# First four attention units: score copies on DVE, results split straight from PSUM, w_out's words queued behind the gates'

## Chip, cores, metric

One Trainium2 chip, one core of it. The metric is the device time of one execution in microseconds; runs are compared by their medians.

## The reference, cut

```python
def _attn_ref(q, k, v, n_sink, window):          # 4 x 8 heads, 768 positions, 64 wide; n_sink 4, window 128
    scores = q @ k.T / sqrt(64), kept where key < n_sink or 0 <= row - key < window
    return softmax(scores) @ v
def _moe_ref(x, w1, w2, w3, w_out):              # x 3072 x 512, gates 512 x 768, w_out 768 x 512
    h = np.maximum(np.maximum(x @ w1, x @ w2), x @ w3)
    return h @ w_out
# then routing of 3072 tokens to 8 experts of 384 each (argsort of all logits), and per expert relu(x @ w1) @ w2
```

## The kernel before

Everything is one instruction stream per engine, laid out by a list scheduler that takes the operations in program order with priorities; each engine then runs its list in order.

**Attention** is cut into 32 units (4 batches, 2 halves of the rows, 4 pairs of heads); four units make a group of 384 tokens. A unit is loaded (`load`), prepared (`prep`), scored (`score`), softmaxed (`soft`) and multiplied with the values (`pv`). The first eight units are "native": their scores are plain fp32 matmuls of queries QF against keys KZ, without the high and low parts of `prep`. In `score` a unit has three blocks of rows and two heads: TensorE (PE) writes a score tile `ps` (three buffers in PSUM), ACT copies it into the score tile T (L134), DVE overwrites the part that the mask selects (L135). The tile for the first block of a first-half unit is preset by POOL (L114) and only DVE writes it (L130, L131). `soft` takes the maximum on DVE (L141), six exponentials on ACT (L144) and scales on POOL (L147, "the weighting"). In `pv`, PE transposes the tile (L25: `pt` for the sink columns, `pp` for the window of each head), DVE multiplies with the triangular masks into A (L163), ACT and DVE split the sink part (`psb`, L153 and L154), and PE accumulates `po` (L170, L172; one buffer). ACT copies `po` to SBUF as x (L173).

**The first mixture** (`Moe1.group`) splits x of each unit into fp32r high and low parts `xh`, `xl` (L267 on ACT, L268 on DVE) and multiplies them with three gates (L280, three products each; maxima on L282 and L283). x2 (L305) multiplies with w_out. The float64 weights arrive as pairs of 32-bit words and are put together by `single` (L220 load, L226 on ACT, L225 and L227 on DVE, L228 on POOL) and split (L212 on ACT, L213 on POOL). The 18 gate pieces pass through a ring of four slots in the storage named HL; the six w_out pieces use two tiles named `st`. Group 0's h is spilled to DRAM and reloaded later by `reload` (L321; split by L323 on ACT and L324 on DVE) before its x2.

Names in rows: until w_out is loaded its storage (`woh`, `wol`) lends room to the attention (`Spare`), so `woh<-in_k_dram` is a native unit's keys and `T_w` or `wol<-ps` is a score tile T. `kz` are the low parts of keys of later, non-native units. SP issues the loads (SPq), in its own order; POOL sets zeros in the unused halves of the key tiles (L53).

The second mixture, with its routing on DVE, begins after about 600 us and is not touched.

Of the kernel before, what the change touches and what calls it, by code (L numbers as in the profile page):

```python
# [22 lines left out]
def f32(ap): return ap.bitcast(FT)  # L23
def flip(nc,out,x,ident):
    nc.tensor.transpose(out,x,f32(ident))  # L25

class Attn:
    def __init__(s, tc, q,k,v,vs, keep, consts, pst, psp, pss, psv, work):
        s.tc=tc; s.nc=nc=tc.nc; s.q,s.k,s.v,s.vs=q,k,v,vs
        s.pst,s.psp,s.pss,s.psv,s.w=pst,psp,pss,psv,work  # L30
        jp=work.tile([128,128],I32,name="jp",tag="qs0",bufs=2)
        nc.gpsimd.iota(jp,pattern=[[1,128]],base=0,channel_multiplier=-1)
        s.ident=keep.tile([128,128],FR,name="ident")
        nc.vector.tensor_scalar(s.ident,jp,0.0,None,op0=OP.is_equal)
        s.ca=consts.tile([128,2,128],U8,name="ca")
        nc.vector.tensor_scalar(s.ca[:,0,:],jp,0.0,None,op0=OP.is_le)
        nc.vector.tensor_scalar(s.ca[:,1,:],jp,0.0,None,op0=OP.is_gt)
        s.ul=consts.tile([128,2,128],BF,name="ul")
        nc.vector.tensor_scalar(s.ul[:,0,:],jp,0.0,None,op0=OP.is_lt)
        nc.vector.tensor_scalar(s.ul[:,1,:],jp,0.0,None,op0=OP.is_ge)  # L40
        s.negs=consts.tile([128,2,4],FT,name="negs"); nc.vector.memset(s.negs,NEG)

        s.vk=[]; s.pb=[]
        for i in range(2):
            t=consts.tile([128,2,128],FR,name=f"vk{i}"); nc.vector.memset(f32(t),0.0); s.vk.append(t)
            t=consts.tile([128,384],FR,name=f"psb{i}"); nc.vector.memset(f32(t),0.0); s.pb.append(t)
        s.kf=[]; s.kz=[s.zeros([consts.tile([128,4,132],FR,name=f"kz{h}") for h in range(2)])]
        t=consts.tile([1,1],FT,name="one"); nc.vector.memset(t,0.0)
        nc.scalar.activation(t,t,AF.Exp)
        s.n=0; s.no=('kh0','kh1')  # L50
        s.extra=None
# [58 lines left out]
    def score(s,u):  # L110
        nc=s.nc; w=s.w; hf=u['hf']
        T=s.two(u,[128,6,132],FT,"T",3)
        u['T']=T
        if hf==0: nc.gpsimd.memset(T[:,0:2,:],NEG)  # L114
        for i in range(3):
            first = hf==0 and i==0
            if first: lo,n=0,132
            else: lo,n=(i-1+hf)*132,260
            t=T[:,2*i:2*i+2,:].rearrange("p u j -> p (u j)")
            for h in range(2):  # L120
                ps=s.pss.tile([128,512],FT,name="ps")
                iq=slice(i*128,(i+1)*128); kz=u['KZ'][h].rearrange("p c j -> p (c j)")[:,lo:lo+n]
                if u['nat']: nc.tensor.matmul(ps[:,:n],u['QF'][:,iq],kz,start=True,stop=True)  # L123
                else:
                    kh=u['KH'][h].rearrange("p c j -> p (c j)")[:,lo:lo+n]
                    nc.tensor.matmul(ps[:,:n],u['QS'][h][:,iq],kh,start=True,stop=False)  # L126
                    nc.tensor.matmul(ps[:,:n],u['QS'][h][:,iq],kz,start=False,stop=True)  # L127
                block=t[:,136*h:136*h+128]; sink=t[:,128+4*h:132+4*h]
                if first:
                    nc.vector.copy_predicated(block,s.ca[:,0,:],ps[:,0:128])  # L130
                    nc.vector.copy_predicated(sink,s.ca[:,1,0:4],ps[:,128:132])  # L131
                else:

                    nc.scalar.activation(t[:,132*h:132*h+132],ps[:,128*h:128*h+132],AF.Copy)  # L134
                    nc.vector.copy_predicated(block,s.ca[:,h,:],ps[:,132-132*h:260-132*h])  # L135
            if hf==0 and i==1:
                nc.vector.copy_predicated(t[:,128:136].rearrange("p (h j) -> p h j",h=2),s.ca[:,1,0:4][:,None,:].to_broadcast([128,2,4]),s.negs)
# [10 lines left out]
    def pv(s,u,x):  # L148
        nc=s.nc; w=s.w; T=u['T'].rearrange('p u j -> p (u j)'); hf=u['hf']; nb=u['nb']; nat=u['nat']
        psk=s.pst.tile([128,512],FT,name="pt")  # L150
        for i in range(3): flip(nc,psk[:,i*128:(i+1)*128],T[:,264*i+128:264*i+256],s.ident)
        PB=s.pb[u['n']%2]
        nc.scalar.activation(PB[0:8],psk[0:8,:384],AF.Copy)  # L153
        nc.vector.tensor_tensor(PB[32:40],psk[0:8,:384],f32(PB[0:8]),op=OP.subtract)  # L154
        jobs=[]
        if hf: jobs.append((0,128,0,0))
        for i in range(3): jobs.append((i*256+128,256 if i<2 else 128,i*128,i+hf))
        for h in range(2):
            pt=s.psp.tile([128,512],FT,name="pp")
            for i in range(3):  # L160
                flip(nc,pt[:,i*128:(i+1)*128],T[:,i*264+136*h:i*264+136*h+128],s.ident)
            A=s.two(dict(n=u['n']*2+h),[128,3,2,128],FT,"A")
            nc.vector.tensor_tensor(A,pt[:,:384].rearrange("p (i q) -> p i q",q=128)[:,:,None,:].to_broadcast([128,3,2,128]),  # L163
                s.ul[:,None,:,:].to_broadcast([128,3,2,128]),op=OP.mult)
            Af=A.rearrange("p i u q -> p (i u q)")
            a=slice(64*h,64*h+64); o=slice(64-64*h,128-64*h)
            if nat:
                if h==0:
                    po=s.psv.tile([128,512],FT,name="po")
                    for a_ in range(2): nc.tensor.matmul(po[:,:384],u['VK'][:,a_,:],PB,start=(a_==0),stop=False,skip_group_check=True)  # L170
                for c,n,q,blk in jobs:
                    nc.tensor.matmul(po[a,q:q+n],u['vn'][:,blk,h,:],Af[:,c:c+n],start=False,stop=True,skip_group_check=True)  # L172
                if h==1: nc.scalar.activation(x,po[:,:384],AF.Copy)  # L173
                continue
            H=w.tile([128,768],FR,name="H"); L=w.tile([128,768],FR,name="L")
            nc.scalar.activation(H,Af,AF.Copy)  # L176
            nc.gpsimd.tensor_tensor(L,Af,f32(H),op=OP.subtract)  # L177
            po=s.psv.tile([128,512],FT,name="po")
            for part in (H,L):
                for j,(c,n,q,blk) in enumerate(jobs):  # L180
                    nc.tensor.matmul(po[:,q:q+n],u['VS'][:,blk,128*h:128*h+128],part[:,c:c+n],start=(part is H and j==0),stop=False,skip_group_check=True)  # L181
            nc.tensor.matmul(po[:,:384],u['VK'][:,h,:],PB,start=False,stop=True,skip_group_check=True)
            nc.scalar.activation(x[a,:],po[o,:384],AF.Copy)
            nc.vector.tensor_tensor(x[a,:],po[a,:384],x[a,:],op=OP.add)

class Spare:

# [15 lines left out]
class Moe1:  # L203
    def __init__(s, tc, words,wgate, consts, wpool, main, conv, mm, pt, pss, ident):
        s.tc=tc; s.nc=tc.nc; s.mm=mm; s.pss=pss; s.main=main; s.conv=conv; s.ident=ident; s.consts=consts
        s.src=words; s.wgate=wgate
        s.W=[[wpool.tile([128,4,768],FR,name=f"w{i}{x}") for x in "hl"] for i in range(3)]
        s.WO=None; s.at=None; s.stage=None; s.HL=None; s.n=0
        s.WG=main.tile([128,6,16],FR,name="wgt")
    def split(s,src,hi,lo):  # L210
        nc=s.nc
# [2 lines left out]
    def single(s,src,ring=False):  # L214
# [2 lines left out]
        if ring and s.stage is None: s.stage=s.main.tile([128,12,384],FT,name="HL").rearrange("p a b -> p (a b)").bitcast(I32)  # L217
        if ring: st=s.stage[:,s.n%4*1024:(s.n%4+1)*1024].rearrange("p (n t) -> p n t",t=2)
        else: st=s.conv.tile([128,512,2],I32,name="st",bufs=2)
        nc.sync.dma_start(st.rearrange("p n t -> p (n t)"),src.bitcast(I32))  # L220
        A=s.pss.tile([128,512],FT,name="ps").bitcast(I32); C=st[:,:,0]
        if ring and s.n%3==2: R=s.stage[:,4096:4608]
        else: R=s.conv.tile([128,512],I32,name="cA",bufs=2)
# [3 lines left out]
        nc.vector.scalar_tensor_tensor(R,st[:,:,1],-0x40000000,A,op0=OP.bitwise_and,op1=OP.bitwise_or)  # L227
        nc.gpsimd.tensor_tensor(R,R,C,op=OP.add)  # L228
        return R.bitcast(FT)
    def part(s,x,f):  # L230
        return s.HL[:,"hl".index(x)*6+f]
    def load_w(s,f):
# [27 lines left out]
    def group(s,xs,spill=None,pool=None,mid=None,between=None):  # L260
# [1 line left out]
        nc=s.nc; main=s.main  # L262
        X=[]
        for p in range(4):
            h=main.tile([128,384],FR,name=f"xh{p}",bufs=1); l=main.tile([128,384],FR,name=f"xl{p}",bufs=1)
            with s.tc.high_priority():
                nc.scalar.activation(h,xs[p],AF.Copy)  # L267
                nc.vector.tensor_tensor(l,xs[p],f32(h),op=OP.subtract)  # L268
            X.append((h,l))
        H=[]  # L270
        if s.HL is None and spill is None: s.HL=main.tile([128,12,384],FR,name="HL")
        for f in range(6):
# [351 lines left out]
def attention_mixtures(tc,q,k,v,vs,words,wg,u1,u2,out,off=60,spread=(0,1,3,4),native=8,order='a0 a0 a0 a0 w a1 w a1 w w a1 w w a1 a2',order1='a2 o o o o o o a2 a2',back=1,at=(1,0),s1=300,s2=400,nring=6):  # L624
    nc=tc.nc
    PS=bass.MemoryType.PSUM
    with ExitStack() as ctx:
# [12 lines left out]
        def att(g,p):  # L640
            xs.setdefault(g,[])
            u=A.load(g//2,g%2,p,4*g+p<native); A.prep(u); A.score(u); A.soft(u)
            x=main.tile([128,384],FT,name=f"x{p}")
            A.pv(u,x); xs[g].append(x)
        def lw(f): M.load_w(f)
        def lo(f): M.load_out(f)
        with tc.block(schedule_with_timeline_sim=True):
            A.extra=Spare(main)
            A.kf=[A.zeros([A.extra.tile([128,4,132],FT,tag=f'kf{i}{h}') for h in range(2)]) for i in range(3)]
            def emit(o,p):  # L650
                n=cnt[o]=cnt.get(o,-1)+1
                if o[0]=='a':
# [136 lines left out]
```

## Time and profile before

| | |
|---|---|
| median of 3 runs | 993.31 us (990.75 to 993.98) |
| the profiled execution: its time, its span | 985.81 us, 984.0 us |
| busy, share of the span | PE 95%, PE weight loads 87%, DVE 70%, ACT 54%, POOL 35% |
| granted TensorE clock, mean | 0.977 |

The span runs from the first to the last instruction of the profiled execution; about 1.8 us lie around it. Busy time of PE counts its time at half clock in full.

### The profile page before, as it was taken

The numbers are of one execution on the slowest core, as the hardware profiler recorded it, in microseconds if no ns is written. First come the engines' busy times: TensorE is split into PE (matmuls) and PEld (weight loads), VectorE is DVE, ScalarE is ACT, GpSimd is POOL, SyncE is SP. The second block draws the span as 40 slices with busy tenths as digits, with TensorE's granted clock in tenths as the row PEclk, the third lists the DMA queues.
The fourth block names the chain that finished last, engine by engine and source line by source line (L and its number), as shares of the span: only waits on it lengthen the run. The fifth ranks groups of instructions, "written<-read, shape, count | busy, mean of one in ns | idle before, by whom it ended". The sixth has DMA issues, their size and how long they took to land.

```text
span 984.0 us, 18469 instructions
## 1 busy us (share of the span) xinstructions
PE 937.8 (95%) x6552; PEld 857.8 (87%) x6552; DVE 687.8 (70%) x1807; ACT 533.8 (54%) x1425; POOL 348.8 (35%) x317
## 2 busy tenths in 40 slices
PE   5889999969999999999999999999999999999996
PEld 4568989959999999999999998888888888888895
DVE  3897676687879976776764344879989889873320
ACT  4666664788789777677663211233433434344431
POOL 3578357145555535425434000011113032043331
PEclk8899999989999999999999999999999999999999
DMA  7455121222112112112110002544345352454420
GB/s 226 151 170 172 50 77 64 68 83 88 53 40 78 52 49 73 28 48 81 64 50 12 1 1 76 164 154 130 119 149 174 98 172 99 160 189 154 135 81 32
DMA packets 50541, 95.03 MB, mean 97 GB/s; under 512 B 6704, under 2 KB 20784, under 8 KB 50448
## 3 DMA queue, kind: packets, MB, share of 16 engines
q1 hardware_dynamic: 40560, 71.57, 23.4%
q0 software_dynamic: 3840, 12.45, 3.6%
q10 hardware_dynamic: 6048, 9.83, 2.7%
q8 instruction: 51, 0.84, 0.4%
q14 instruction: 42, 0.34, 0.1%
HBM read 77.84 MB, written 16.12 MB: 95 GB/s over the span
## 4 chain that ended last, share of the span: by engine, by line
PE 75%; DVE 8%; ACT 6%; issue 5%; DMA 4%; POOL 1%; SPq 1%; POOLq 0%; ACTq 0%; DVEq 0%
PE mm L280 28%; PE mm L608 11%; PE acc L601 11%; PE mm L305 7%; PE po L181 3%; PE rc L406 2%; PE pt L25 2%; PE pp L25 2%; PE po L172 2%; PE ps L126 1%; PE ps L127 1%; DMA sa<-in_u_dram 1%; PE ps L123 1%; DVE A_w L163 1%; DVE qs L97 1%
## 5 line engine op out<-in xcount | busy, mean ns | idle before, releaser
L601 PE MATMUL acc<-wbh,HL 128*128 128x512 f32 x384 | 131.1, 398 | 0.0
L177 POOL TENSOR_TENSOR L<-A_w,H 128x768 fp32r<-128x768 f32 x46 | 87.0, 1891 | 101.5 <-ACT H L176 91.1
L283 DVE TENSOR_TENSOR hm<-mm,hm 128x384 f32<-128x384 f32 x96 | 53.3, 555 | 68.6 <-PE mm L280 65.1
L620 POOL DMA_INDIRECT out_dram<-og,idx x24 | 32.2, 1340 | 180.6 <-ACT og L619 177.3
L305 PE MATMUL mm<-woh,HL 128*128 128x260 f32 (+1 forms) x432 | 89.5, 296 | 2.0 <-DVE HL L324 1.1
L552 ACT ACTIVATE wah<-sa 128x512 fp32r<-128x512 f32 x64 | 40.5, 632 | 89.6 <-PE mm L608 72.2
L601 PEld LDWEIGHTS acc<-wbh,HL 128*128 128x128 f32 x384 | 71.5, 188 | 12.8
L552 ACT ACTIVATE wbh<-sb 128x512 fp32r<-128x512 f32 x64 | 40.4, 631 | 74.9 <-PE acc L601 72.0
L601 PE MATMUL acc<-wbl,HL 128*128 128x512 f32 x192 | 76.9, 401 | 0.0
L305 PEld LDWEIGHTS mm<-woh,HL 128*128 128x128 f32 x432 | 72.3, 198 | 3.3 <-DVE HL L324 1.4
L608 PE MATMUL mm<-HL,wah 128*128 128x384 f32 x256 | 68.5, 343 | 0.0
L280 PE MATMUL mm<-xh,w0h 128*128 128x384 f32 x192 | 66.8, 348 | 1.2 <-ACT xh L267 0.6
L280 PE MATMUL mm<-xh,w1h 128*128 128x384 f32 x192 | 66.7, 347 | 0.8 <-ACT hm L282 0.5
L280 PE MATMUL mm<-xl,w0h 128*128 128x384 f32 x192 | 65.5, 341 | 1.9 <-DVE xl L268 1.9
L280 PE MATMUL mm<-xh,w2h 128*128 128x384 f32 x192 | 67.0, 349 | 0.0
L280 PE MATMUL mm<-xh,w1l 128*128 128x384 f32 x192 | 65.5, 341 | 0.0
L280 PE MATMUL mm<-xl,w2h 128*128 128x384 f32 x192 | 65.5, 341 | 0.0
L553 DVE TENSOR_TENSOR wbl<-sb,wbh 128x512 fp32r<-128x512 f32 x64 | 43.9, 688 | 30.7 <-ACT wbh L552 30.7
L280 PE MATMUL mm<-xl,w1h 128*128 128x384 f32 x192 | 65.1, 339 | 0.0
L280 PE MATMUL mm<-xh,w0l 128*128 128x384 f32 x192 | 65.1, 339 | 0.0
L280 PE MATMUL mm<-xh,w2l 128*128 128x384 f32 x192 | 65.1, 339 | 0.0
L612 DVE SCALAR_TENSOR_TENSOR HL<-mm,HL 128x384 fp32r<-128x384 f32 x64 | 35.5, 554 | 40.8 <-ACT HL L611 40.6
(320 smaller groups left out, 2888.3 us busy)
## 6 DMA issues: line engine op xcount, KB each, us to landing
sa<-in_u_dram SPq DMA_DIRECT2D x64, 256.0 KB
sb<-in_u_dram SPq DMA_DIRECT2D x64, 256.0 KB
HL<-in_words_dram SPq DMA_DIRECT2D x18, 512.0 KB
qn<-in_q_dram SPq DMA_DIRECT2D x24, 192.0 KB
x2d<-xo ACTq DMA_DIRECT2D x15, 256.0 KB
kn<-in_k_dram SPq DMA_DIRECT2D x12, 264.0 KB
st<-in_words_dram SPq DMA_DIRECT2D x6, 512.0 KB
vn<-in_v_dram SPq DMA_DIRECT2D x12, 256.0 KB
```

The source lines that it names most:

```text
L25: nc.tensor.transpose(out,x,f32(ident))
L177: nc.gpsimd.tensor_tensor(L,Af,f32(H),op=OP.subtract)
L181: nc.tensor.matmul(po[:,q:q+n],u['VS'][:,blk,128*h:128*h+128],part[:,c:c+n],start=(part is H and j==0),stop=False,skip_group_check=True)
L280: nc.tensor.matmul(ps[:,:384],s.W[i][a][:,p,f*128:(f+1)*128],X[p][b],start=(n==0),stop=(n==11)); n+=1
L283: else: nc.vector.tensor_tensor(m,ps[:,:384],m,op=OP.max)
L305: nc.tensor.matmul(ps[:,:n],H[f][a][:,t*128:(t+1)*128],s.WO[b][:,f,u,c],start=(k==0),stop=(k==17)); k+=1
L552: nc.scalar.activation(h,src,AF.Copy)
L553: (nc.gpsimd if s.n>=6 and nm=="wa" else nc.vector).tensor_tensor(l,src,f32(h),op=OP.subtract)
L601: s.mms.append(nc.tensor.matmul(acc[t],H[f][a][:,t*128:(t+1)*128],W[f][1][b],start=(f==0 and n==0),stop=(f==F-1 and n==2))); n+=1
L608: s.mms.append(nc.tensor.matmul(ps[:,:384],W[f][0][a][:,k,:],X[k][b],start=(n==0),stop=(n==11))); n+=1
L612: nc.vector.scalar_tensor_tensor(l,ps[:,:384],0.0,f32(h),op0=OP.max,op1=OP.subtract)
L620: st=nc.gpsimd.indirect_dma_start(out=s.out,out_offset=bass.IndirectOffsetOnAxis(ap=idx[:,t:t+1],axis=0),in_=o,in_offset=None)
```

## The change

Native units 0 to 3 (`u['n']<4`, all of group 0's units) have their score copies on DVE. `pv` gets a list of results: for group 0 it is the pair of tiles (`xh`, `xl`), and `split` fills it from `po` directly, ACT the high and DVE the low part; `group` then finds the pair ready. Other groups keep x in SBUF and split as before. A w_out piece's load is ordered behind the gate load that is sixth from the last (the 13th). The zeros of `kz` are set after those of the native key tiles instead of before.

```diff
+def split(nc,hl,x):
+    nc.scalar.activation(hl[0],x,AF.Copy)
+    nc.vector.tensor_tensor(hl[1],x,f32(hl[0]),op=OP.subtract)
...
-        s.kf=[]; s.kz=[s.zeros([consts.tile([128,4,132],FR,name=f"kz{h}") for h in range(2)])]
+        s.kf=[]; s.kz=[[consts.tile([128,4,132],FR,name=f"kz{h}") for h in range(2)]]
...
-                    nc.scalar.activation(t[:,132*h:132*h+132],ps[:,128*h:128*h+132],AF.Copy)
+                    if u['n']<4: nc.vector.tensor_copy(t[:,132*h:132*h+132],ps[:,128*h:128*h+132])
+                    else: nc.scalar.activation(t[:,132*h:132*h+132],ps[:,128*h:128*h+132],AF.Copy)
...
-                if h==1: nc.scalar.activation(x,po[:,:384],AF.Copy)
+                if h==1:
+                    for c in x: split(nc,c,po[:,:384]) if type(c) is tuple else nc.scalar.activation(c,po[:,:384],AF.Copy)
...
-        nc.sync.dma_start(st.rearrange("p n t -> p (n t)"),src.bitcast(I32))
+        ld=nc.sync.dma_start(st.rearrange("p n t -> p (n t)"),src.bitcast(I32))
+        if ring: s.loads.append(ld)
+        else: s.tc.add_manual_dep(ld.ins,s.loads[-6].ins.name,mybir.DependencyInfo(mybir.DependencyClass.NoSync,mybir.DependencyReason.DATA),reason="order of loads")
...
+    def pair(s,p):
+        return tuple(s.main.tile([128,384],FR,name=f"x{x}{p}",bufs=1) for x in "hl")
...
-            h=main.tile([128,384],FR,name=f"xh{p}",bufs=1); l=main.tile([128,384],FR,name=f"xl{p}",bufs=1)
-            with s.tc.high_priority():
-                nc.scalar.activation(h,xs[p],AF.Copy)
-                nc.vector.tensor_tensor(l,xs[p],f32(h),op=OP.subtract)
-            X.append((h,l))
+            if type(xs[p]) is tuple: X.append(xs[p]); continue
+            X.append(s.pair(p))
+            with s.tc.high_priority(): split(nc,X[p],xs[p])
...
-            x=main.tile([128,384],FT,name=f"x{p}")
-            A.pv(u,x); xs[g].append(x)
+            x=main.tile([128,384],FT,name=f"x{p}") if g else M.pair(p)
+            A.pv(u,[x]); xs[g].append(x)
...
+            A.zeros(A.kz[0])
```

The scheduler lays every list out anew, and rows move on all engines. In the rows of the changed kernel the line numbers are higher (L134 is L138 on DVE for group 0 and L139 on ACT, L226 is L234, L142 to L147, L144 to L149, L163 to L168, L324 to L332).

Three places follow. The first is the start of the program, on SP and on ACT. SP's list there, before and then changed (`vns` are a unit's four sink values, `woh` and `wol` with 64x396 the halves of its keys):

```order
7 L71 DMA qf<-in_q_dram 128x384
8 L79 DMA vnn<-in_v_dram 128x384
9 L81 DMA vns<-in_vs_dram 40x128
10 L69 DMA woh<-in_k_dram 64x396
11 L69 DMA wol<-in_k_dram 64x396
12 L220 DMA HL<-in_words_dram 128x1024
```
```order
7 L75 DMA qf<-in_q_dram 128x384
8 L83 DMA vnn<-in_v_dram 128x384
9 L73 DMA woh<-in_k_dram 64x396
10 L73 DMA wol<-in_k_dram 64x396
11 L85 DMA vns<-in_vs_dram 40x128
12 L226 DMA HL<-in_words_dram 128x1024
```

The third unit's two key loads have moved ahead of the second unit's sink values.

ACT's list at the same place, before and changed (`HL<-HL` is the scaling of a gate piece, `m`, `T_w,l`, `l` belong to the softmax):

```order
4 L134 ACTIVATE T_w<-ps 128x132 x4
5 L226 ACTIVATE HL<-HL 128x512
6 L134 ACTIVATE T_w<-ps 128x132
7 L142 ACTIVATE m<-m 128x6
8 L134 ACTIVATE T_w<-ps 128x132
9 L144 ACTIVATE T_w,l<-T_w,m 128x132 x6
10 L134 ACTIVATE T_w<-ps 128x132 x2
11 L226 ACTIVATE HL<-HL 128x512
12 L145 ACTIVATE l<-l 128x6
```
```order
4 L234 ACTIVATE HL<-HL 128x512
5 L147 ACTIVATE m<-m 128x6
6 L149 ACTIVATE T_w,l<-T_w,m 128x132 x6
7 L234 ACTIVATE HL<-HL 128x512
8 L150 ACTIVATE l<-l 128x6
```

The score copies are gone from between the scaling and the softmax; the scaling now stands first.

The second place is PE's list where the first unit's transposes begin, before and changed (rows `ps<-woh,qf 128x132` at this place are the fourth unit's first scores):

```order
11 L123 MATMUL ps<-wol,qf 128x260
12 L123 MATMUL ps<-woh,qf 128x132 x2
13 L25 MATMUL pt<-ident,T_w 128x128 x3
14 L25 MATMUL pp<-ident,T_w 128x128 x6
15 L123 MATMUL ps<-woh,qf 128x260 x2
16 L170 MATMUL po<-psb_105,vk_103 128x384 x2
17 L172 MATMUL po<-A_w,vnn 64x256 x2
```
```order
11 L127 MATMUL ps<-wol,qf 128x260
12 L25 MATMUL pt<-ident,T_w 128x128 x3
13 L25 MATMUL pp<-ident,T_w 128x128 x3
14 L127 MATMUL ps<-woh,qf 128x132 x2
15 L127 MATMUL ps<-woh,qf 128x260
16 L25 MATMUL pp<-ident,T_w 128x128 x3
17 L175 MATMUL po<-psb_105,vk_103 128x384 x2
```

The transposes of the sink part and of the first head now stand ahead of the fourth unit's first scores; those of the second head still stand behind them.

The third place is DVE's list where group 0's h is reloaded, before and changed, the last three of six splits (`HL<-hm`):

```order
294 L324 TENSOR_TENSOR HL<-hm,HL 128x384 x2
295 L135 COPY_PREDICATED T_w<-ca,ps 128x128
296 L184 TENSOR_TENSOR x_1672<-po,x_1672 64x384
297 L135 COPY_PREDICATED T_w<-ca,ps 128x128 x2
298 L163 TENSOR_TENSOR A_w<-pp,ul 128x768
299 L324 TENSOR_TENSOR HL<-hm,HL 128x384 x2
```
```order
312 L332 TENSOR_TENSOR HL<-hm,HL 128x384
313 L140 COPY_PREDICATED T_w<-ca,ps 128x128
314 L99 TENSOR_TENSOR kz0b<-kn,kh_x 64x528
315 L140 COPY_PREDICATED T_w<-ca,ps 128x128
316 L99 TENSOR_TENSOR kz1b<-kn,kh_x 64x528
317 L140 COPY_PREDICATED T_w<-ca,ps 128x128
318 L146 TENSOR_REDUCE m<-T_w 128x6
319 L101 TENSOR_TENSOR qs_2972<-qn,qs_2972 64x384
320 L332 TENSOR_TENSOR HL<-hm,HL 128x384
```

Before, the fifth and the sixth split stand side by side; now seven rows of a later unit's preparation stand between them.

## Rows read from the trace of the kernel before

**Rows 1.** Windows: busy us by engine (instructions), PE clock, DMA share, GB/s

```profile
0.00:10.00 10.00, 5.17 (x15) 4.15 (x16) 4.37 (x20) 2.61 (x6) 7.00 (x20) 1.00 0.47 137
10.00:25.00 15.00, 9.88 (x33) 6.34 (x31) 5.33 (x21) 9.91 (x41) 1.52 (x2) 0.74 0.94 288
25.00:45.00 20.00, 15.78 (x65) 10.11 (x65) 17.16 (x33) 13.11 (x46) 10.03 (x11) 0.77 0.47 143
45.00:65.00 20.00, 16.34 (x83) 11.12 (x83) 17.54 (x33) 13.83 (x45) 16.03 (x15) 1.00 0.54 177
65.00:125.00 60.00, 60.00 (x339) 53.45 (x338) 45.78 (x89) 37.91 (x119) 39.89 (x39) 0.97 0.35 117
198.00:225.00 27.00, 18.77 (x103) 16.37 (x102) 23.99 (x40) 23.73 (x74) 13.51 (x9) 0.76 0.31 90
```

**Rows 2.** The chain that ended last, 5 to 66 us: start, us, what

```profile
7.47 0.31 SPq L81
...
8.97 3.99 DMA HL<-in_words_dram
...
12.98 0.65 ACT HL L226
...
14.93 7.42 DMA qf<-in_q_dram
...
25.02 0.96 DVE A_w L163
...
30.73 3.25 PE po L172 x11
...
62.78 1.70 DVE xl L268
```

**Rows 3.** ACT in order of time: start, us, line, operation [idle before, releaser]

```profile
17.26 0.67 ACT L226 ACTIVATE HL<-HL 128x512 int32<-128x512 uint32 x1 [0.51 <-DMA HL<-in_words_dram]
...
60.84 0.49 ACT L173 ACTIVATE x<-po 128x384 f32<-128x384 f32 x1 [0.62 <-PE po L172]
```

**Rows 4.** PE in order of time, from the fourth unit's first scores

```profile
22.49 1.22 PE L123 MATMUL ps<-woh,qf 128*128 128x132 f32 x4 [0.53 <-DMA qf<-in_q_dram]
23.50 0.85 PE L25 MATMUL pt<-ident,T_w 128*128 128x128 f32 x3
...
26.04 0.90 PE L25 MATMUL pp<-ident,T_w 128*128 128x128 f32 x3 [1.05 <-DVE A_w L163]
26.73 1.07 PE L123 MATMUL ps<-woh,qf 128*128 128x260 f32 x2
...
29.52 1.21 PE L170 MATMUL po<-psb,vk 128*128 128x384 f32 x2
```

**Rows 5.** POOL in order of time

```profile
5.84 0.57 POOL L114 MEMSET T_w<- 128x264 f32 x2
...
7.00 0.45 POOL L102 TENSOR_TENSOR vk<-vns,vk 40x128 fp32r<-40x128 f32 x1
...
18.33 1.51 POOL L147 TENSOR_TENSOR T_w<-T_w,l 128x792 f32<-128x792 f32 x1 [8.32 <-DVE l L146]
```

**Rows 6.** DVE's groups, 0 to 66 us: busy us, mean ns, idle before

```profile
L268 DVE TENSOR_TENSOR xl<-x,xh 128x384 fp32r<-128x384 f32 x4 | 5.4, 1345 | 1.3 <-ACT xh L267 1.2
L135 DVE COPY_PREDICATED T_w<-ca,ps 128x128 f32<-128x128 uint8 x18 | 5.0, 298 | 4.4 <-ACT T_w L134 4.3
...
L154 DVE TENSOR_TENSOR psb<-pt,psb 8x384 fp32r<-8x384 f32 x4 | 2.2, 547 | 0.1
```

**Rows 7.** DVE around the reload, 190 to 226 us, in order of time

```profile
212.63 0.55 DVE L324 TENSOR_TENSOR HL<-hm,HL 128x384 fp32r<-128x384 f32 x1
213.77 0.56 DVE L324 TENSOR_TENSOR HL<-hm,HL 128x384 fp32r<-128x384 f32 x1 [0.59 <-ACT HL L323]
...
215.66 1.91 DVE L95 TENSOR_TENSOR kz0b<-kn,kh_x 64x528 fp32r<-64x528 f32 x1 [0.36 <-ACT kh_x L94]
...
219.38 0.70 DVE L95 TENSOR_TENSOR kz1b<-kn,kh_x 64x528 fp32r<-64x528 f32 x1
```

More of the change, by code (lines that the diff above doesn't have):

```diff
@@ L182, in pv @@
             nc.tensor.matmul(po[:,:384],u['VK'][:,h,:],PB,start=False,stop=True,skip_group_check=True)
-            nc.scalar.activation(x[a,:],po[o,:384],AF.Copy)
-            nc.vector.tensor_tensor(x[a,:],po[a,:384],x[a,:],op=OP.add)
+            nc.scalar.activation(x[0][a,:],po[o,:384],AF.Copy)
+            nc.vector.tensor_tensor(x[0][a,:],po[a,:384],x[0][a,:],op=OP.add)
 class Spare:
@@ L207, in __init__ @@
         s.W=[[wpool.tile([128,4,768],FR,name=f"w{i}{x}") for x in "hl"] for i in range(3)]
-        s.WO=None; s.at=None; s.stage=None; s.HL=None; s.n=0
+        s.WO=None; s.at=None; s.stage=None; s.HL=None; s.n=0; s.loads=[]
         s.WG=main.tile([128,6,16],FR,name="wgt")
```

## The prediction, as put on record

> **What bounds it now.** I read the windows first [rows 1]. From 65 us PE is busy for all of 60 us at a clock of 0.97, and it stays near that to the end but for one stretch, 198 to 225, with 18.77 busy of 27 at 0.76. So after 65 us the time is PE's work, and a change that keeps PE's work can win only in two places: the start, and that stretch. [...] From 25 to 65 us DVE is the fullest other engine (34.7 of 40), before that DMA is (share 0.94).
>
> Next the chain through the start [rows 2]. SP waits to 7.47 for POOL to have read the first unit's sink values (L102, 7.00 plus 0.45 [rows 5]); behind that load stand two key loads and then the first gate piece, issued at 8.97. Its data releases ACT's scaling at 12.98. Two of the second unit's score copies, and the first unit's softmax, stand behind that scaling. The score copies hold up PE, whose scores of the second unit free the buffer for the fourth unit's queries; that load goes out at 14.93 behind three more gate pieces and lands 7.42 us later. PE starts the fourth unit's scores at 22.49 and only then, at 23.50, the first unit's transposes [rows 4], though the weighting that feeds them ended at 18.33 + 1.51 = 19.84 [rows 5]. A follows at 25.02, the value products from 30.73 to 33.98, and the fourth unit's xl ends at 64.48 [rows 2]; there PE becomes full.
>
> **The change, term by term.**
>
> *1. The first unit arrives earlier: -5.0 us.* (a) The third unit's key loads no longer stand behind SP's wait. They filled 7.78 to 8.97, so the first gate piece goes out about 1.1 us earlier; DMA is not full by then (0.47 over the first 10 us [rows 1]), so ACT's scaling comes about 1.0 earlier. (b) No score copy stands between it and the softmax, 0.1 to 0.2 us more. ACT then still waits for the second piece (17.26 now [rows 3]), which moves by about 1 us with the first. The weighting so ends near 18.7 instead of 19.84. (c) PE takes the transposes ahead of the fourth unit's scores: first A at about 20.2 (18.7 plus the 1.5 that lie between 23.50 and 25.02 now) instead of 25.02. (d) The second head's transposes still stand behind those scores. Their queries land at most 1 us earlier, because the same bytes go ahead of them on full DMA engines [rows 1]. Landing at 21.3, then 1.22 and one score of 1.07, gives 23.6 instead of 26.04 [rows 4]. (e) `po` starts at 29.52 now, because L154, which it needs, waits in DVE's list long after the transposes of the sink part (23.50); in the new order L154 stands right behind the first A. The second A then ends near 25.3 (23.6, the transposes 0.65, A 0.96 [rows 2, 4]), and with the 3.25 us of the value products these end at 28.5 to 29 instead of 33.98. Bounds: -2.4 if only (d) holds, -6.5 if nothing holds the second A.
>
> *2. The last unit's result is split at once: -2.4 us.* Now it takes 60.84 [rows 3] to 64.48 [rows 2], 3.6 us: a copy of 0.49, a wait for ACT, the high part, and a DVE subtraction of 1.70. From PSUM it is the high part (ACT, about the 0.49 of the copy) and a DVE subtraction like L154, which also reads PSUM, 0.55 [rows 6]: 1.2 us with the hop. Bounds: -1.2 (ACT late all the same) and -2.4. DVE's four L268 take 1345 ns each [rows 6], so it gains 3.2 us of room in all, of which I count only this unit's. The one `po` buffer is held until DVE is through, up to 0.6 us longer than by the copy; the next unit's product behind it waits for its own transposes and A anyway, and without that cover it would be 0.6 for each of three units.
>
> [...]
>
> *3. The copies on DVE: +1.0 us.* 16 copies of 128x132; not in the trace on DVE. The nearest row, a masked copy of 128x128 from PSUM, takes 298 ns [rows 6]: 4.8 us. Those of three units lie before 25 us, where DVE is busy 9.7 of 25 [rows 1]; they also save the hop to ACT, for which DVE idled 4.3 us [rows 6]. Those of the fourth unit, 4 x 0.3, lie in the full stretch. Bounds: 0 and 2.4 (half of them).
>
> [...]
>
> *4. w_out's words: 0.* Two pieces of 0.5 MB that ACT scaled before 32 us now load between the 13th and 14th gate piece. If they stood fully in the way, 1.05 MB at the 288 GB/s of the second window would be 3.6 us; but after 65 us the DMA share is 0.35 [rows 1], and the gate pieces wait for ring slots. What hides it is PE's backlog of attention and gate products.
>
> *5. Zeros: 0.* POOL sets as many tiles as before ahead of T's memset at 5.84 [rows 5], for which DVE's first score waits. PE may start up to 1.1 us earlier and then waits for DVE.
>
> *6. The stretch 198 to 225: 0, bounds -4 and +4.* DVE (23.99 of 27) and ACT (23.73) set it [rows 1], with work that the change leaves alone but for its order.
>
> Sum: -5.0 - 2.4 + 1.0 = -6.4. What PE gains at 65 us it keeps to 198 if it is fed: POOL, which makes the gates' low parts, is busy 16.03 of 20 and 39.89 of 60 us [rows 1], so it can come earlier by as much. The profiled execution, 985.8 us with 1.8 outside the span, would come to 979.4; the three timed runs have a median of 993.31, 7.5 us above it, and the difference taken from that gives **986.8 us**.
>
> **Rivals.** *A, more (982).* All four units chain. DVE idled 4.3 us for score copies in the first 66 us [rows 6], and the three other L268 take 5.4 - 1.7 = 3.7 us that become 3 x 0.55, if DVE is what the units wait for. With -6.5 for term 1, -4.4 for term 2 and 0 for 3 it is -10.9, or 982.4. Against it: the second unit's words and the fourth's queries still come by DMA.
>
> *B, DMA still sets the pace (990.8).* The fourth unit's queries land when the bytes ahead of them have moved, and half of every result of the first unit waits for them: only (d), -2.4 to -2.5. For it: DMA share 0.94. Against it: L154 waits on DVE, not on data.
>
> *C, given back (992.8).* PE reaches 198 to 225 earlier, but DVE and ACT do not: they are 88% full there, and a lead of PE alone is used up by waiting longer. Against it: the second engines also run earlier, and DVE was busy 45.78 of 60 before.
>
> *D, slower (997).* The last reload split. Before, the fifth and sixth stand side by side, 212.63 and 213.77 [rows 7]. Now two key splits (1.91 and 0.70 [rows 7]), three masked copies, a maximum and a query split stand between them, about 5 us on a DVE that works at 89% there. PE's x2 takes the pieces in turn and waits. The wait adds some 4 us. If the clock falls to half for all of the stretch's busy time, 18.77 x (0.76/0.5 - 1) = 9.8 us come on top. It decides once the stretch is over 9.4 us longer: from there the total is over 996.3. I put it at 10 to 11 longer. Against it: as much DVE work then lies behind the sixth split less, where PE waits now (215 to 222).
>
> **Chances.** Forecast (-4 to -9) 0.40, A 0.18, B 0.15, C 0.17, D 0.10. About 3 us, 0.3%, is what a measurement of this kernel tells from no change (the three runs span 3.2). Faster by more: nearly all of the forecast (0.37), A (0.18), two fifths of B (0.06), a little of C (0.02): 0.63. Slower: most of D (0.09) and some of C (0.04): 0.13. Same: 0.24. The range 981.0 to 993.8 takes in the forecast with its bounds, A without a better late stretch, B and most of C, and leaves out D and the ends: about 0.83. The forecast's own range is 984 to 989.5.
>
> **What would show it.** Right: the first transposes near 19 us, the first gate piece's scaling near 12, the fourth unit's xl ending near 58, and PE full from there; 198 to 225, moved by the lead, as long as before. Term 1 is wrong if the first unit's value products still end after 31; term 2 if xl still takes over 1 us; term 3 if DVE is full before 25 us. Wrong altogether if PE's idle time in the first 65 us falls by 6 us and the total does not: then look at the stretch of the reload for C or D.

## The result and the profile after

The change makes the kernel slower: 1007.28 us (median of five, 1001.59 to 1009.98) against 993.98 (median of five), ratio 1.0137 (95%: 1.0116 to 1.0157). The profiled execution has a span of 1005.5 us, 21.5 more than before's; some 7.5 of these are there because before's profiled execution was that much quicker than its median (see "Noise").

The start came forward much as forecast. First the windows of the changed kernel, columns as in [rows 1], with the two that lie behind it:

```profile
0.00:10.00 10.00, 5.07 (x16) 4.12 (x16) 5.53 (x24) 1.49 (x2) 6.27 (x18) 1.00 0.61 176
10.00:25.00 15.00, 8.94 (x35) 5.96 (x35) 11.07 (x35) 9.12 (x37) 2.24 (x3) 0.83 0.85 248
25.00:45.00 20.00, 16.57 (x86) 11.40 (x85) 15.54 (x38) 12.19 (x44) 13.25 (x15) 0.95 0.42 131
45.00:65.00 20.00, 18.34 (x93) 13.84 (x92) 17.80 (x35) 14.83 (x51) 16.74 (x17) 1.00 0.58 187
65.00:125.00 60.00, 58.07 (x335) 50.83 (x333) 44.83 (x87) 37.52 (x110) 36.67 (x37) 1.00 0.37 123
198.00:225.00 27.00, 22.54 (x148) 20.51 (x147) 19.62 (x39) 24.96 (x79) 12.24 (x9) 0.87 0.25 79
225.00:300.00 75.00, 67.49 (x424) 66.00 (x423) 64.21 (x105) 53.81 (x150) 35.73 (x34) 0.93 0.18 49
300.00:525.00 225.00, 215.85 (x1457) 211.26 (x1457) 166.78 (x303) 162.75 (x488) 94.00 (x79) 0.99 0.18 56
```

The same last two windows of the kernel before:

```profile
225.00:300.00 75.00, 74.35 (x516) 73.39 (x514) 58.80 (x119) 62.24 (x185) 37.60 (x34) 1.00 0.19 56
300.00:525.00 225.00, 221.94 (x1500) 217.49 (x1500) 163.80 (x303) 164.61 (x479) 104.70 (x88) 1.00 0.18 57
```

In the first 65 us PE's idle time (65 less its busy time in the four windows) is 16.1 us instead of 17.8, and the clock from 10 to 45 us 0.83 and 0.95 instead of 0.74 and 0.77 [rows 1]. Then the loss: from 225 to 525 us PE does 1881 matmuls where it did 2016, with 283.3 us busy instead of 296.3.

PE in order of time, where [rows 4] stood:

```profile
20.61 0.90 PE L25 MATMUL pt<-ident,T_w 128*128 128x128 f32 x3 [0.42 <-POOL T_w L152]
...
23.09 2.08 PE L127 MATMUL ps<-woh,qf 128*128 128x132 f32 x6 [0.94 <-DMA qf<-in_q_dram]
24.97 0.84 PE L25 MATMUL pp<-ident,T_w 128*128 128x128 f32 x3
25.47 0.99 PE L175 MATMUL po<-psb,vk 128*128 128x384 f32 x2
...
27.78 0.60 PE L177 MATMUL po<-wol,vnn 128*64 128x256 f32 x3
```

The scaling of the first two gate pieces on ACT, in order of time as in [rows 3], and DVE's first A, which stood at 25.02 in [rows 2]:

```profile
11.37 0.66 ACT L234 ACTIVATE HL<-HL 128x512 int32<-128x512 uint32 x1 [8.86 <-DMA HL<-in_words_dram]
...
18.00 0.65 ACT L234 ACTIVATE HL<-HL 128x512 int32<-128x512 uint32 x1 [3.34 <-DMA HL<-in_words_dram]
```

```profile
22.24 0.95 DVE L168 TENSOR_TENSOR A_w<-pp,ul 128x768 f32<-128x768 f32 x1
```

Three of these places in a second profile of the changed kernel (after_again below): the scaling of the second piece on ACT, and the transposes of the two heads on PE:

```profile
16.42 0.65 ACT L234 ACTIVATE HL<-HL 128x512 int32<-128x512 uint32 x1 [1.89 <-DMA HL<-in_words_dram]
```

```profile
19.04 0.90 PE L25 MATMUL pt<-ident,T_w 128*128 128x128 f32 x3
...
23.61 0.85 PE L25 MATMUL pp<-ident,T_w 128*128 128x128 f32 x3
```

DVE's groups over the whole span (for [rows 6]), its last split of group 0, and its rows around the reload (for [rows 7]):

```profile
L29 DVE TENSOR_TENSOR xl<-x,xh 128x384 fp32r<-128x384 f32 x28 | 21.6, 800 | 1.6 <-ACT xh L28 1.5
...
L138 DVE COPY T_w<-ps 128x132 f32<-128x132 f32 x12 | 3.4, 290 | 1.0 <-PE ps L127 0.9
L29 DVE TENSOR_TENSOR xl<-po,xh 128x384 fp32r<-128x384 f32 x4 | 2.2, 550 | 0.1
```

```profile
56.97 0.55 DVE L29 TENSOR_TENSOR xl<-po,xh 128x384 fp32r<-128x384 f32 x1
```

```profile
209.27 0.69 DVE L332 TENSOR_TENSOR HL<-hm,HL 128x384 fp32r<-128x384 f32 x1 [0.21 <-ACT HL L331]
210.08 0.69 DVE L99 TENSOR_TENSOR kz0b<-kn,kh_x 64x528 fp32r<-64x528 f32 x1
211.61 0.71 DVE L99 TENSOR_TENSOR kz1b<-kn,kh_x 64x528 fp32r<-64x528 f32 x1 [0.37 <-ACT kh_x L98]
...
214.37 0.56 DVE L332 TENSOR_TENSOR HL<-hm,HL 128x384 fp32r<-128x384 f32 x1
```

For that last piece PE waits 0.82 us:

```profile
214.99 0.51 PE L313 MATMUL mm<-woh,HL 128*128 128x260 f32 x2 [0.82 <-DVE HL L332]
```

Two places show what the loss is made of. PE near 124 and near 237 us:

```profile
127.16 0.69 PE L288 MATMUL mm<-xh,w0h 128*128 128x384 f32 x1 [3.16 <-ACT xh L28]
```

```profile
236.66 0.39 PE L130 MATMUL ps<-kh_x,qs 128*128 128x260 f32 x1 [0.61 <-DVE T_x L140]
...
239.79 0.58 PE L130 MATMUL ps<-kh_x,qs 128*128 128x260 f32 x1 [2.62 <-DVE T_x L140]
...
240.39 0.53 PE L288 MATMUL mm<-xh,w2h 128*128 128x384 f32 x1
...
244.23 0.42 PE L130 MATMUL ps<-kh_x,qs 128*128 128x260 f32 x1
```

Near 237 us the score matmuls stand in PE's list ahead of the twelve gate matmuls w2h. The scores need a buffer that a mask on DVE (L140) frees, and that mask stands behind a key split of 2.18 us; POOL works on L183 during 1.75 us of it. DVE, then POOL:

```profile
237.22 2.18 DVE L99 TENSOR_TENSOR kz<-kn,kh_w 64x396 fp32r<-64x396 f32 x1
239.44 0.30 DVE L140 COPY_PREDICATED T_x<-ca,ps 128x128 f32<-128x128 uint8 x1
```

```profile
237.13 1.84 POOL L183 TENSOR_TENSOR L<-A_w,H 128x768 fp32r<-128x768 f32 x1 [3.31 <-ACT H L182]
```

And the price is paid twice: PE stands for 3.2 us, and the clock falls from 1.00 to 0.85 and 0.50 (that the wait brings this about is not shown). PE's windows of 5 us:

```profile
230.00:235.00 5.00, 5.00 (x37) 4.90 (x36) 2.76 (x3) 4.03 (x9) 3.74 (x4) 1.00 0.09 11
235.00:240.00 5.00, 1.77 (x11) 1.29 (x10) 4.81 (x8) 3.13 (x8) 1.84 (x1) 0.85 0.16 48
240.00:245.00 5.00, 5.00 (x18) 5.00 (x19) 4.21 (x9) 3.02 (x15) 0.00 (x0) 0.50 0.29 80
```

At 0.50 the twelve gate matmuls take 3.84 us (240.39 to 244.23); the next twelve, at 1.00, take 2.08 (246.05 to 248.13).

### The profile page after: what moved, and what is told of

Read it like the earlier page. It is cut to its first block, busy times and chain, and to the rows that moved or that the text cites. A ratio compares the mean times of both kernels' runs of the same rounds, so it can differ in the third digit from the quotient of the medians.

```text
span 1005.5 us, 18457 instructions
## 1 busy us (share of the span) xinstructions
PE 941.2 (94%) x6552; PEld 861.1 (86%) x6552; DVE 701.8 (70%) x1823; ACT 528.2 (53%) x1405; POOL 344.0 (34%) x317
## 4 chain that ended last, share of the span: by engine, by line
PE 69%; DVE 9%; ACT 8%; issue 7%; DMA 5%; POOL 1%; SPq 1%; POOLq 0%; ACTq 0%; DVEq 0%
PE mm L288 26%; PE mm L616 11%; PE acc L609 11%; PE mm L313 6%; PE po L187 3%; PE rc L414 2%; PE pt L25 2%; DMA qf<-in_q_dram 2%; PE pp L25 1%; DVE qs L101 1%; PE ps L127 1%; ACT T_w L149 1%; DMA sa<-in_u_dram 1%; PE ps L130 1%; PE ps L131 1%
## 5 line engine op out<-in xcount | busy, mean ns | idle before, releaser
L183 POOL TENSOR_TENSOR L<-A_w,H 128x768 fp32r<-128x768 f32 x46 | 87.0, 1892 | 103.6 <-ACT H L182 93.0
L313 PE MATMUL mm<-woh,HL 128*128 128x260 f32 (+1 forms) x432 | 87.3, 291 | 5.1 <-DVE HL L297 1.5
L313 PEld LDWEIGHTS mm<-woh,HL 128*128 128x128 f32 x432 | 69.9, 191 | 7.3 <-DVE HL L297 1.9
```

The source lines that it names most:

```text
L313: nc.tensor.matmul(ps[:,:n],H[f][a][:,t*128:(t+1)*128],s.WO[b][:,f,u,c],start=(k==0),stop=(k==17)); k+=1
```

## The experiments

**How far ahead.** For every run the table gives PE's lag behind the first profile of before at five marks (minus: ahead). It is worked out from counts: matmuls in windows of 25 us are summed; the time at which a kernel reaches the count that before had at the mark, less the mark. The changed kernel has 1311 matmuls at 250 us and 131 more by 275; before had 1318 at 250: 250 + 25 x 7/131 = 251.3, a lag of 1.3. Units stand in another order and a few records are missing, so I trust the count to some 2 us. A profile is also one execution: start_after_order_before and order_held_again are the same kernel and differ by 4.5 us at 550, and the profiles of words_alone and all_but_split_order_held are the quickest of their four runs. The last columns are the difference of the medians and the ratio; the ratio is not that of the two medians and can differ from it (copies_order_held: 4.0 us by the medians, 0.9942 or 5.8 us by the ratio, 3.7 to 7.7 by its interval). The kernel before itself took 993 us on most chips and 984.7 on the one that ran the second group; each ratio is against before on the same chip.

| run | 75 | 150 | 250 | 400 | 550 | median, us | ratio (95%) |
|---|---|---|---|---|---|---|---|
| the changed kernel | -8.5 | -2.3 | 1.3 | 14.1 | 13.6 | +13.3 | 1.0137 (1.0116 to 1.0157) |
| after_again | -9.4 | -2.0 | 4.0 | 16.0 | 15.3 | +14.3 | 1.0131 (1.0099 to 1.0162) |
| start_after_order_before | -10.0 | -6.6 | -5.8 | -5.7 | -6.1 | -2.6 | 0.9987 (0.9967 to 1.0006) |
| order_held_again | -8.4 | -2.1 | -1.6 | -1.2 | -1.6 | -1.8 | 0.9982 (0.9959 to 1.0005) |
| start_before_order_after | -0.7 | 7.0 | 10.3 | 21.6 | 20.4 | +19.4 | 1.0196 (1.0159 to 1.0233) |
| split_alone | -5.9 | 0.3 | -2.0 | 8.8 | 14.3 | +14.9 | 1.0152 (1.0130 to 1.0173) |
| all_but_split | 1.4 | 2.6 | 4.6 | 4.4 | 3.8 | +4.4 | 1.0045 (1.0018 to 1.0071) |
| before_rows_860_1559 | -10.0 | -3.5 | 2.9 | 7.2 | 7.0 | +11.6 | 1.0134 (1.0094 to 1.0174) |
| before_rows_450_730 | -9.4 | 3.2 | 10.6 | 24.0 | 22.4 | +23.0 | 1.0226 (1.0185 to 1.0267) |
| zeros_alone | 0.4 | 0.3 | 0.9 | 7.3 | 10.9 | +9.4 | 1.0094 (1.0069 to 1.0119) |
| before_again | 0.0 | 0.9 | 0.6 | 1.2 | 0.7 | +1.6 | 1.0017 (0.9998 to 1.0036) |
| split_order_held | -4.1 | -0.4 | -0.1 | -0.3 | -0.5 | -0.2 | 0.9989 (0.9972 to 1.0006) |
| copies_order_held | -6.5 | -4.3 | -3.6 | -2.8 | -3.3 | -4.0 | 0.9942 (0.9922 to 0.9963) |
| copies_alone | -5.8 | 1.5 | 4.2 | 8.6 | 14.0 | +14.0 | 1.0145 (1.0128 to 1.0162) |
| words_alone | -4.6 | 0.0 | 0.5 | 6.8 | 3.5 | +7.8 | 1.0087 (1.0065 to 1.0109) |
| all_but_split_order_held | 0.2 | 0.3 | 1.6 | 1.4 | 1.4 | +5.4 | 1.0059 (1.0041 to 1.0076) |

The changed kernel is 8.5 us ahead at 75 us and 13.6 behind at 550. TensorE's list in the two kernels differs in 2869 of 3459 rows of the scheduled block, the last at row 3134 (some 520 us); behind it they are alike. Theory 1: the edits do what they were meant to, and the new order of all later units costs more. Rival: the edits cost later by themselves.

**Start and order exchanged.** TensorE's list from row 250 on is held to a written table; the other engines' lists then follow it closely.

```diff
+def pin(tc,eng,table):
...
+        n+=int(d); i=ins[n]
+        if last is not None: tc.add_manual_dep(i,last.name,mybir.DependencyInfo(mybir.DependencyClass.NoSync,mybir.DependencyReason.DATA),reason="order of before")
+        last=i
...
+            pin(tc,mybir.EngineType.PE,ORDER_PE)
         wpool.release()
```

> The changed kernel in full; only TensorE's list from its row 250 on (some 75 us into the span) is held to the order that it has in the kernel before. Theory 1 (the start gains some 7 us as the edits intend, and the loss comes from the new order in which the scheduler lays out all later units): 984 to 990 us, ahead of the kernel before by 4 to 9 us, and TensorE idle between 225 and 525 us falls from 16.7 us to under 8. Rival (the edits themselves cost later: a buffer held longer, w_out's words late, a fuller VectorE): still 1002 to 1010 us.

> The kernel before in full, without any of the four edits; only TensorE's list from its row 250 on is held to the order that it has in the changed kernel. Theory 1 (the later order costs): 1005 to 1018 us, slower than the changed kernel itself, since the gain of the start is missing. Rival (the edits cost): 990 to 997 us, as the kernel before.

Both crossings follow the order, not the edits: 0.9987 with the new start and the old order, 1.0196 with the old start and the new order. The second is also some 6 us slower than the changed kernel (1.0137 and 1.0131), as theory 1 expected: even under the new order the new start is worth some 6 us, with wide intervals. The first kernel's windows beside those above, then the second's:

```profile
225.00:300.00 75.00, 73.33 (x508) 72.27 (x507) 61.68 (x124) 62.43 (x182) 39.37 (x38) 1.00 0.19 57
300.00:525.00 225.00, 222.54 (x1496) 218.11 (x1496) 161.56 (x296) 161.19 (x469) 102.83 (x86) 1.00 0.18 55
```

```profile
225.00:300.00 75.00, 66.86 (x431) 65.40 (x432) 60.23 (x96) 54.73 (x164) 38.46 (x34) 0.93 0.17 51
300.00:525.00 225.00, 216.69 (x1476) 212.88 (x1476) 168.38 (x311) 163.80 (x481) 100.58 (x85) 1.00 0.18 57
```

PE's idle time from 225 to 525 us falls to 4.1 us in the first, as theory 1 asked. The rival is out as the main cause. But 0.9987 is less than theory 1 asked for, so the first kernel ran once more, with the changed kernel beside it.

> The changed kernel with TensorE's list of before from row 250 on, once more and beside the changed kernel itself: its first profile was 6 us ahead of before from 75 to 575 us, but its median only 2.6 us. Theory 1 (the start's gain is kept when the order is held): 0.993 to 0.996 of before, 6 us ahead at 575 us again. Rival (the second mixture takes back what arrives early): 0.996 to 0.999, with TensorE's waits for th after 575 us longer than in a profile of before on the same chip.

> The changed kernel once more, on the same chip as the three runs beside it, since the kernel before took 993 us on one chip and 985 us on another. If its loss is made by 575 us (13.6 us at the 550 us mark of its first profile) it costs the same on any chip: 12 to 15 us over before, 1.012 to 1.015.

The changed kernel repeats its loss. The held one is 8.4 us ahead at 75, 3.4 at 100 and 1.6 at 550: its lead went between 85 and 95 us, at a wait of PE of 2.29 us and a low clock behind it (0.66 from 90 to 95 us).

```profile
90.69 0.68 PE L127 MATMUL ps<-woh,qf 128*128 128x260 f32 x2 [2.29 <-ACT qs L100]
```

Its first profile has the same wait of 2.29 us, but the clock stayed at 1.00, and it kept 6 us to 550. The windows from 90 to 95 us, second profile, then first:

```profile
90.00:95.00 5.00, 4.31 (x15) 4.29 (x16) 3.12 (x5) 4.26 (x18) 4.33 (x4) 0.66 0.40 143
```

```profile
90.00:95.00 5.00, 5.00 (x29) 4.82 (x29) 2.93 (x9) 4.83 (x21) 5.00 (x5) 1.00 0.01 2
```

The medians say 2.6 and 1.8 us, and neither interval excludes no change. By its number the second run (0.9982) falls to the rival of its expectation, but in its profile the lead is gone before the second mixture begins. So the held order removes the loss; how much of the start's lead it keeps is not settled.

**Parts alone, order free.** Each is the kernel before with only that part of the change's diff (all_but_split has the other three).

> The kernel before with one of the four parts: results of group 0 split straight from PSUM. Theory 1: the time of a re-laid order can't be worked out from the edit; since the order differs from that of before in most of the rows up to 520 us, 990 to 1012 us, with the first 65 us shorter by 2 to 4 us. Rival (the part that costs is this one, xh and xl being held from the end of the unit on): 1002 to 1010 us, with waits for these two tiles or for x in the rows.

> The changed kernel without the direct split (copies on VectorE, w_out's words ordered and zeros moved stay). TensorE's list is that of the kernel before from some 300 us on. Theory 1: 986 to 995 us, since from there on nothing differs. Rival (copies on VectorE or late words cost): 1000 to 1008 us.

> The kernel before with one edit that by itself costs and gives nothing: the zeros of the first K tiles are set first. TensorE's list is re-laid in its first 250 rows and again from row 800 on. Theory 1 (any edit re-lays the later order, and the time follows that order): a time other than that of before by more than 0.3%, on the slow side more likely: 994 to 1010 us. Rival (only edits that do something cost): 990 to 995 us.

> The kernel before with the score copies of the first four units on VectorE alone, its order left to the scheduler; 2660 of 3459 rows of TensorE's list in the block then differ from before. With the order held the same edit took 0.994 of before. If a re-laid order costs by itself, whatever edit re-lays it: 1.000 to 1.015. If only some edits' orders are bad (the split's, the zeros'), this one may come out at 0.990 to 0.998.

> The kernel before with the order of w_out's loads alone, order left to the scheduler; 2774 rows of TensorE's list differ from before. The forecast gave this edit nothing. If a re-laid order costs by itself: 1.003 to 1.015. If not: 0.998 to 1.002.

Four edits, four re-laid lists, and each alone is slower by 0.9 to 1.5%, also the two that I had costed at nothing. Why none of the four came out faster is not shown. zeros_alone is level with before until 250 us and loses 10 us after that, in rows that the edit does not touch. For the split alone the rival's own sign is small: in the first 150 us PE waits 3.4 us for xh and 0.5 for xl, yet it is 5.9 us ahead at 75 and still 2.0 at 250; the loss comes after that. all_but_split, whose list is that of before from some 300 us on, loses nothing after 250. Its expectation of 986 to 995 failed all the same (997.5): it starts late, see below.

**Parts alone, order held** by the same table:

> The kernel before with the direct split alone, and TensorE's list held to that of before from row 250 on. By the forecast's term 2: 2.4 us (bounds 1.2 and 4.4) faster than before, 0.9955 to 0.999. Without the held order this part alone cost 14.9 us; if that cost were the part's own and not the order's, it would stay at 1.01 or more.

> The kernel before with the score copies of the first four units on VectorE alone, TensorE's list held to that of before from row 250 on. By the forecast's terms 1 and 3, as far as the copies make them (the transposes come ahead of the fourth unit's scores): 2 to 4 us faster, 0.996 to 0.998. Rival (VectorE is the fuller engine and loses what ScalarE gains): 0.999 to 1.003.

> The changed kernel without the direct split, TensorE's list held to that of before from row 250 on. Beside the copies (0.994 alone) it has w_out's words behind the gates' and the zeros first. If these two add to the start: 0.990 to 0.994, the best version so far; if they are worth nothing, as the forecast has it, 0.993 to 0.996; 0.996 or more if the words, loaded late, hold something up.

The copies give 4.0 us with the order held and cost 14.0 with it free: same edit, 2% apart. copies_order_held beats both kernels and is the best version found; its 0.9942 is better than the 0.996 to 0.998 expected. For the split, 0.9989 lies in the expected range, but its interval takes in both no change and the full 2.4 us, so its worth is not settled. Its profile is 4.1 us ahead at 75, 1.7 at 100 and 0.4 at 150; one wait of 1.76 us is the part of this that a row shows. PE in that kernel:

```profile
93.13 0.68 PE L127 MATMUL ps<-woh,qf 128*128 128x260 f32 x2 [1.76 <-ACT HL L254]
```

Before has no wait from 66 to 108 us, nor has copies_order_held; order_held_again waits 2.29 us for ACT at the same scores. In split_order_held's chain of waits ACT's x copy, the high part of a gate piece and a scaling stand ahead of those scores. I take it that PE came earlier and this work on ACT did not; no run separates it. all_but_split_order_held has lost its lead by 75 us already, in the rows that the table does not hold:

```profile
59.87 0.69 PE L306 MATMUL mm<-xh,w0h 128*128 128x384 f32 x1 [4.40 <-ACT xh L293]
62.40 0.90 PE L25 MATMUL pt<-ident,T_w 128*128 128x128 f32 x3 [1.53 <-POOL T_w L148]
```

ACT's rows in that kernel say what came before the longer wait:

```profile
53.59 0.67 ACT L252 ACTIVATE HL<-HL 128x512 int32<-128x512 uint32 x1 [2.31 <-DMA HL<-in_words_dram]
...
59.30 0.52 ACT L293 ACTIVATE xh<-x 128x384 fp32r<-128x384 f32 x1
```

ACT stands for the words of a gate piece, issued at 49.16, then takes a unit's six exponentials, and only then copies and splits the x that PE needs. The words of w_out are issued later, at 67.00, so it is not them that PE waits for. The result falls in the expectation's third range (0.996 or more), but this wait does not show its reason, that late words hold something up. So the parts don't add: with copies and split both, words and zeros do no such harm. Which of the two edits puts ACT's rows in this order was not tried.

**Part of the order.** Can the loss be taken back place by place? The changed kernel with its own list, but for one stretch of it as in before (a table of both):

> The changed kernel with its own list on TensorE, but for rows 860 to 1559 (some 176 to 290 us), which stand as in the kernel before. Theory 1 (the loss sits in the places where the new list puts score matmuls that wait ahead of gate matmuls that could run): between the 175 us mark and the 300 us mark the changed kernel fell from 1.8 us ahead of before to 7.2 us behind; this list takes that back: 996 to 1001 us, and the wait of 2.6 us for a score buffer near 237 us is gone. Rival (the changed start hands on some lateness that any order must pay): 1003 to 1009 us, the idle time reappearing at other rows.

> The changed kernel with its own list on TensorE, but for rows 450 to 730 (some 108 to 157 us), which stand as in the kernel before. Theory 1: between 100 and 150 us the changed kernel lost 5 us of its lead, with a wait of 3.2 us for the high part of x near 124 us and half clock after it; this list takes that back: 1000 to 1004 us, that wait gone. Rival: 1005 to 1010 us, the wait standing elsewhere.

Neither did. From 225 to 300 us the first has its idle time down to 0.3 us and the wait near 237 us is gone, as expected, but ahead of it stands a new wait, for POOL's weighting. In the second the wait for xh is gone too, and a new wait for the weighting stands in its own stretch; its 1.0226 is the largest ratio of all. The longest waits of PE from 65 to 575 us in the first, then the second:

```profile
PE pt L25 <- POOL T_w L152: 10.3, 2, 6.0
```

```profile
PE pt L25 <- POOL wol L152: 7.3, 1, 7.3
```

The 996.3 us of the first lies in the expected range only because that chip was quicker; its ratio is that of the changed kernel. In both, the list of TensorE spliced from two made waits of its own. Which places in the new order cost how much is therefore not settled; that the order as a whole costs it, is.

**Noise.** 

> The kernel before once more, for a second profile of it: its profiled execution took 985.81 us, 7.5 us less than the median of its runs. If the routing and expert stages (after 575 us) vary from run to run, this profile shows them longer, with TensorE's waits for th above the 2.1 us of the first profile; ratio to before 1.000 within 0.002.

The second profile of before runs level with the first within 1.2 us at these marks; the expectation of longer stages after 575 us failed. The 7.5 us between the first profile and the median are probably a matter of the chip (below): on the quick chip the kernel before ran in 982.1 to 990.1 us, on the three others never under 988.8. On which chip that profile was taken is not known.

## Why the prediction was wrong

**The step that failed** is the sentence "What PE gains at 65 us it keeps to 198 if it is fed", with the price of 0 for the order behind it. PE was not fed, busy 58.07 of the 60 us from 65 on and 283.3 of the 300 from 225 on: the lead of 8.5 us at 75 was 2.3 at 150 and a lag of 14.1 at 400, since the units' instructions stood in another order on every engine. I priced a changed order only for the reload (rival D and term 6), not for the 400 us around it. The sum has no term for what the order costs: +15 us with the new start (1.0131 and 1.0137 against 0.9982 and 0.9987), +19 with the old. (A slip besides: 993.31 less the sum's 6.4 is 986.9, not 986.8.)

**Term 1** (-5.0) was right in most steps: scaling at 11.37 (forecast near 12), value products done at 28.38 (28.5 to 29). Between them the profiled execution ran 1 to 2 us late. The first transposes came at 20.61 (19) and A at 22.24 (20.2), because the second gate piece did not come earlier with the first (18.00 after 17.26). The second head's transposes came at 24.97 (23.6), because the fourth unit's scores waited for their queries to 23.09. The second profile has 16.42, 19.04 and 23.61 for the piece and the two transposes, as forecast, so the lateness belongs to the transfers of one execution. The value products made it good: they started at 25.47, before the second A (25.85 to 26.81) and not behind it.

**Term 3** (+1.0) was right in size: 16 copies at 290 and 275 ns where I took 298. Terms 1 and 3 together were to give 4.0, and with the order held the copies gave 4.0 by the medians, 5.8 by the ratio. That the first figure is met is in part luck: that kernel scales the first gate piece at 12.78, so step (a) is hardly in it, and its profile was 6.5 us ahead at 75 and 3.3 at 550.

**Term 2** (-2.4) was right at its place: xl from PSUM takes 0.55 and the fourth unit's ends at 57.52 (forecast 58). Its worth for the total stays open: with the order held 0.2 us by the medians, 1.1 by the ratio, from 2.8 faster to 0.6 slower by its interval. No run shows the 4.4 that rival A counts for it; it lies outside that interval.

**Terms 4 and 5** (0 and 0) were wrong as the kernel is built: +7.8 and +9.4 us with the order free. Neither adds an operation of that length; each re-lays the list, and zeros_alone is level until 250 us. Neither was run alone with the order held.

**Term 6, C and D.** The stretch 198 to 225 became better, 22.54 busy at 0.87 instead of 18.77 at 0.76, though in the new order it also holds other work. D's order came as foreseen, 5.1 us between the last two splits, but PE waited 0.82 for it, not 4. The sign was D's, the mechanism not. The sign named last (PE's idle time down by 6 us, the total not) did not come in that form: the idle time fell by 1.7 us, and the rest of the lead at 75 us goes with the higher clock from 10 to 45 us (0.83 and 0.95 instead of 0.74 and 0.77). It would also have sent the reader to the wrong stretch, since the loss grows from 225 us on.

## What to carry to other kernels

Where a list scheduler lays out the whole program, an edit at the start is two edits: its own, and a new order for everything behind it. Cost the second too, or hold the order fixed, measure the edit, and only then let the scheduler loose. Here the held order turned the same copies from 1.4% slower into 0.4 to 0.6% faster.

## What the runs showed of the hardware

The DVE subtraction L99, with two SBUF inputs, took longer at some places beside POOL: in the changed kernel 522 to 2181 ns, the longest from 237.22 on beside POOL's L183 above. The seven L99 over 1 us all run beside a tensor operation of POOL for 0.8 us or more; the other 41 took at most 0.71 us. The 28 xl from SBUF took 543 to 2868 ns, the four from PSUM 547 to 556, with POOL's tensor operations beside them for 0.39 us at most. Near 237 us the mask that PE waited 2.62 us for stood behind the L99 of 2181 ns.

Chips differ: before took 984.7 us on one and 993 on three others. split_order_held, within 1 us of before's first profile from 200 to 600 us, is 8.7 behind at 950, with the same list in that stage. PE's wait for the routing's th there, in before_again (quick chip) and in split_order_held:

```profile
PE rc L406 <- DVE th L401: 2.5, 4, 1.0
```

```profile
PE rc L434 <- DVE th L429: 8.1, 6, 2.4
```

Why was not tried.
